# GpSimd takes a subtraction of the weight loads, ScalarE takes the spreading of reciprocal sums

## The chip, the cores and the metric

The kernel runs on one core of one Trainium2 chip. The metric is the device time of one execution in microseconds (us). Three runs of the kernel before took 1221.29 to 1222.41 us, with a median of 1221.92 us; the lower, the better.

## The reference

The reference is an attention with a learned bias, followed by two feed-forward layers. All in fp32:

```python
scores = q @ k.T / sqrt(64) + bias          # 4 batches x 8 heads, 576 x 576
attn   = exp(scores - max) / (sum + 1e-09)  # row by row
x      = (attn @ v)                         # laid out as 2304 tokens x 512
h = x @ w_in;  x = (h * clip(h + 3, 0, 6) / 6) @ w_out           # 2048 wide
x = (sigmoid(x @ w_gate) * (x @ w_val)) @ w_out2                 # 1536 wide
```

The bias is a small network of the distance of two positions. It is made once, for all batches.

## The kernel before, in words

The program has three stages: the table of the bias (to about 60 us of the span), the attention (about 60 to 356 us), and the two feed-forward layers (the rest). The change touches the attention alone, through two pieces of work that sit inside it.

**The attention** goes over 16 units (`NU`): a unit is a pair of heads of one batch. Each unit has 9 steps of 128 query rows, and `slot_of_two` issues two steps at a time. For a step, TensorE forms the scores (L261). VectorE adds the bias and finds each row's minimum (L265, the tile `u`). ScalarE takes the exponential and, with it, the sum of each row (L281, `p` or `pm`, with the sums in `stat`). TensorE transposes the probabilities (L319, L327, L334, `tr`), VectorE and ScalarE by turns copy the result out of PSUM (`ptm`, `ptr`), and TensorE multiplies by the values (L351, L354, `av`).

**The reciprocal sums.** The output comes out transposed, so the sums have to be turned too. `invert` does this in two parts per unit, after step 5 and after step 8. VectorE adds 1e-9 to the sums (L287) and takes reciprocals (L288). GpSimd then repeats each column of reciprocals 64 or 128 times into the tile `spread` (L292, by a multiplication with a column of ones): one instruction of 128x384 in the first part, two of 128x128 in the second. `turn_inv` has TensorE transpose `spread` (L298), and copies the result to `inv`. At L358 VectorE multiplies the output by `inv` and so frees the PSUM tile `av` for the next product.

**Keys and queries.** `prep` splits the next unit's queries and keys into a high part and a remainder. GpSimd makes the high part of the keys (L233) and the remainders of both (L237); ScalarE makes the high part of the queries (L229).

**Weight loads.** The feed-forward weights come as eight-byte numbers and are made into two parts, a high one and a low one, each in a slot of 128x512. `Loader.whole` runs a whole load at once. It is called ten times in the attention (`NPRE` is 10), at every sixth slot. A load is a DMA, then ScalarE's L133, then VectorE's L134, L141, L143 and L145, then `split`: ScalarE rounds the high part into the slot (L151), and VectorE subtracts it to get the low part (L152). Later loads go through `tick`, with the same `split`.

Each engine works through its own queue strictly in order. The framework sets the order inside each queue, from its own estimates of when each operand is ready; it differs from the order of the source.

Of the kernel before, what the change touches and what calls it, by code (L numbers as in the profile page):

```python
# [10 lines left out]
F32 = mybir.dt.float32  # L11
# [3 lines left out]
ALU = mybir.AluOpType  # L15
# [80 lines left out]
def block_kernel(ctx: ExitStack, tc: tile.TileContext, q, k, v, mlp, w_in, w_out, w_gate, w_val, w_out2, dist_d,  # L96
                 rows_d, out):
    nc = tc.nc
# [7 lines left out]
    one = keep.tile([P, 1], F32, name="one")  # L106
# [5 lines left out]
    class Loader:  # L112
# [32 lines left out]
            nc.vector.scalar_tensor_tensor(out=zi, in0=raw[:, :, 0], scalar=29, in1=zi,  # L145
                                           op0=ALU.logical_shift_right, op1=ALU.bitwise_or)

        def split(self, i):
            if i in self.z:
                slot, z = slots[i % NALL], self.z.pop(i)  # L150
                nc.scalar.copy(slot[:, 0], z)  # L151
                nc.vector.tensor_tensor(out=slot[:, 1], in0=z, in1=slot[:, 0].bitcast(F32), op=ALU.subtract)  # L152
                self.done = i + 1

        def whole(self):
            i = self.n
            for stage in (self.dma, self.magnitude, self.assemble, self.split):
                stage(i)
            self.n += 1

        def tick(self):
# [122 lines left out]
    def invert(n, c0, c1):  # L284

        r = sums[n % 3][:, 2 * c0 : min(2 * c1, NSTEP)]
        nc.vector.tensor_scalar(out=r, in0=r, scalar1=1e-9, scalar2=None, op0=ALU.add)  # L287
        nc.vector.reciprocal(r, r)  # L288
        for s0, s1, w in ((0, 6, 64),) if c1 == 3 else ((6, 8, 64), (8, 9, P)):
            o = spread[:, 64 * s0 : 64 * s0 + (s1 - s0) * w].rearrange("p (s w) -> p s w", w=w)  # L290
            i = sums[n % 3][:, s0:s1].unsqueeze(2).to_broadcast(o.shape)
            nc.gpsimd.tensor_tensor(out=o, in0=i, in1=one.unsqueeze(2).to_broadcast(o.shape), op=ALU.mult)  # L292

    def turn_inv(n, c0, c1):

# [70 lines left out]
    for n in range(NU):  # L366
        i = (NSTEP * n + 5) // 2 + 2
# [8 lines left out]
    def slot_of_two(i):  # L376
# [15 lines left out]
        for t in steps(i - 1):  # L392
            n, s = seq[t]
            if s in (5, 8):
                invert(n, s // 6 * 3, s // 6 * 2 + 3)
# [22 lines left out]
    with ExitStack():  # L418
# [215 lines left out]
        for j, (part2, t) in enumerate(todo):  # L634
# [25 lines left out]
            for i in range(NB):  # L660
                o = acc[NB * t + i]
# [32 lines left out]
```

## Time and profile before

| | |
|---|---|
| three runs | 1221.29 to 1222.41 us, median 1221.92 us |
| the profiled execution | 1220.53 us |
| its span, first to last instruction | 1218.8 us |
| TensorE busy | 1193.4 us (98%) |
| VectorE busy | 694.6 us (57%) |
| ScalarE busy | 563.2 us (46%) |
| GpSimd busy | 147.9 us (12%) |
| granted TensorE clock | 1.00 throughout |

Shares are over the whole span. TensorE's busy time is modelled from pipelined matmuls, so 98% does not mean that nothing can be gained. VectorE and ScalarE are much busier in the attention than their averages say, and GpSimd works in the attention alone. PE stands for TensorE, PEld for its loading of weights, DVE for VectorE, ACT for ScalarE, POOL for GpSimd, SP for the queue that issues DMAs.

### The profile page before, as it was taken

Reading aid. Unit: us, or ns where it says so; the run is one execution under the profiler, and the core shown is the slowest. Engines: PE = TensorE matmul, PEld = TensorE weight load, DVE = VectorE, ACT = ScalarE, POOL = GpSimd, SP = SyncE. Lnnn points to the kernel's source line nnn. Section 1 sums busy time; section 2 is a strip of 40 time slices with the busy share of each in tenths; the row PEclk is TensorE's granted clock in tenths of the full one; section 3 lists DMA queues with packets and bytes.
Section 4 is the critical chain, followed back from the end, with each engine's and each line's share of the span. In section 5 each row is a group of like instructions: output and inputs, shape, how many; then the busy total and the mean of one; then the engine's idle time right before and its main releaser. Section 6 shows DMA issues by size and latency. Waiting matters only on the chain.

```text
span 1218.8 us, 18824 instructions
## 1 busy us (share of the span) xinstructions
PE 1193.4 (98%) x7302; PEld 1059.3 (87%) x7302; DVE 694.6 (57%) x1474; ACT 563.2 (46%) x1176; POOL 147.9 (12%) x146
## 2 busy tenths in 40 slices
PE   8999999999999999999999999999999999999998
PEld 4467767676679999999999999999999999999998
DVE  8967887878867665645555555555442454313332
ACT  7977777676755443444443434233322332212221
POOL 0056546546300000000000000000000000000000
PEclk9999999999999999999999999999999999999999
DMA  6743536234312332212122222322210121001000
GB/s 211 251 137 98 179 88 186 86 110 141 98 36 87 104 104 78 67 38 78 49 91 104 104 87 90 126 82 75 79 43 19 61 79 53 31 21 53 26 26 27
DMA packets 36154, 106.78 MB, mean 88 GB/s; under 512 B 3936, under 2 KB 10336, under 8 KB 36064
## 3 DMA queue, kind: packets, MB, share of 16 engines
q1 hardware_dynamic: 36064, 105.57, 26.5%
q8 instruction: 57, 0.93, 0.3%
q14 instruction: 33, 0.27, 0.1%
HBM read 80.78 MB, written 24.77 MB: 87 GB/s over the span
## 4 chain that ended last, share of the span: by engine, by line
PE 85%; DVE 6%; ACT 3%; POOL 2%; issue 2%; DMA 1%; SPq 0%; DVEq 0%; POOLq 0%; ACTq 0%
PE o L573 16%; PE h L511 13%; PE h L509 13%; PE h L510 13%; PE o L630 12%; PE s L261 5%; PE av L351 5%; PE tr L319 4%; PE s L488 2%; PE av L354 1%; DVE x L483 1%; DVE u L265 1%; PE tr L298 1%; ACT p L281 1%; POOL k L237 1%
## 5 line engine op out<-in xcount | busy, mean ns | idle before, releaser
L509 PE MATMUL h<-early,slot 128*128 128x384 f32 x952 | 318.9, 335 | 0.0
L511 PE MATMUL h<-early,slot 128*128 128x384 f32 x952 | 318.8, 335 | 0.0
L510 PE MATMUL h<-early,slot 128*128 128x384 f32 x952 | 318.5, 335 | 0.0
L509 PEld LDWEIGHTS h<-early,slot 128*128 128x128 f32 x952 | 178.7, 188 | 2.6
L510 PEld LDWEIGHTS h<-early,slot 128*128 128x128 f32 x952 | 178.7, 188 | 2.5
L511 PEld LDWEIGHTS h<-early,slot 128*128 128x128 f32 x952 | 178.6, 188 | 0.1
L550 ACT CAST gh<-g 128x384 fp32r<-128x384 f32 x166 | 85.0, 513 | 160.1 <-DVE g L645 119.0
L573 PE MATMUL o<-gh,slot 128*128 128x384 f32 x768 | 156.9, 336 | 1.9 <-ACT raw L309 1.4
L645 DVE TENSOR_TENSOR g<-g,h 128x384 f32<-128x384 f32 x72 | 39.8, 553 | 181.8 <-PE h L511 181.8
L573 PEld LDWEIGHTS o<-gh,slot 128*128 128x128 f32 x768 | 134.2, 188 | 5.7 <-ACT raw L309 4.1
L551 DVE TENSOR_TENSOR gl<-g,gh 128x384 fp32r<-128x384 f32 x166 | 92.1, 558 | 78.4 <-ACT gh L550 76.2
L515 ACT ACTIVATE g<-h,half 128x384 f32<-128x384 f32 x94 | 54.5, 580 | 133.4 <-PE h L511 129.9
L261 PE MATMUL s<-k,q 128*128 128x288 f32 x640 | 113.9, 311 | 1.6 <-POOL k L237 1.0
L281 ACT ACTIVATE p<-u,stat 128x576 f32<-128x576 f32 x128 | 98.7, 772 | 36.1 <-DVE stat L265 35.3
L630 PE MATMUL o<-slot,gh 128*128 128x512 f32 x432 | 111.9, 393 | 0.0
L644 ACT ACTIVATE g<-h 128x384 f32<-128x384 f32 x72 | 35.4, 492 | 163.2 <-PE h L511 163.1
L516 DVE SCALAR_TENSOR_TENSOR g<-g,h 128x384 f32<-128x384 f32 x94 | 51.8, 551 | 96.9 <-ACT g L515 96.9
L265 DVE CUSTOM_DVE_ANT_0 u<-s,bias 128x576 f32<-128x576 f32 x128 | 93.7, 752 | 13.1 <-PE s L261 12.2
L261 PEld LDWEIGHTS s<-k,q 128*128 128x128 f32 x640 | 89.7, 189 | 6.6 <-DVE stat L265 3.0
L630 PEld LDWEIGHTS o<-slot,gh 128*128 128x128 f32 x432 | 80.1, 188 | 13.6 <-issue 0.2
L573 PE MATMUL o<-gl,slot 128*128 128x384 f32 x384 | 88.5, 334 | 0.0
L351 PE MATMUL av<-ptm,vn 128*64 128x288 f32 x512 | 82.8, 419 | 0.5 <-DVE ptm L311 0.5
(98 smaller groups left out, 1509.0 us busy)
## 6 DMA issues: line engine op xcount, KB each, us to landing
raw<-in_part_dram SPq DMA_DIRECT2D x68, 512.0 KB, 3.6
nbias<-p SPq DMA_DIRECT2D x18, 576.0 KB, 3.2
early<-in_part_dram SPq DMA_DIRECT2D x32, 288.0 KB, 4.2
bias<-nbias SPq DMA_DIRECT2D x16, 576.0 KB, 5.9
take<-x SPq DMA_DIRECT2D x12, 768.0 KB, 4.1
vn<-in_part_dram SPq DMA_DIRECT2D x16, 320.0 KB, 3.0
early<-in_part_dram SPq DMA_DIRECT2D x16, 304.0 KB, 3.8
part<-raw SPq DMA_DIRECT2D x12, 384.0 KB, 2.6
```

The lines of the kernel that those rows point to most:

```text
L261: nc.tensor.matmul(ps[:, a, 0:HS], Q[:, q0 : q0 + P], K[:, r, h, HS * a : HS * a + HS], start=(i == 0), stop=(i == len(mm) - 1))
L265: last_u[0] = nc.vector.tensor_tensor_reduce(out=halves(u), in0=ps[:, :, 0:HS], in1=halves(bt), op0=ALU.add, op1=ALU.min, scale=-0.125, sc ...
L281: nc.scalar.activation(probs(t), us.pop(t), AF.Exp, bias=low[n % 2][:, s : s + 1], scale=-1.0, accum_out=sums[n % 3][:, s : s + 1])
L351: nc.tensor.matmul(ps[64 * h : 64 * h + 64, 0:HS], vt[:, 4 * h + g], ptm[:, h, g, cols], start=(g == 0), stop=False)
L509: nc.tensor.matmul(ps[:, 0:TW], wh, XH[:, c], start=(c == 0), stop=False)
L510: nc.tensor.matmul(ps[:, 0:TW], wl, XH[:, c], start=False, stop=False)
L511: nc.tensor.matmul(ps[:, 0:TW], wh, XL[:, c], start=False, stop=(c == 3))
L515: nc.scalar.activation(g, ph, AF.Relu, bias=half, scale=1.0 / 6.0)
L550: nc.scalar.copy(gh, g)
L551: last_g[0] = nc.vector.tensor_tensor(out=gl, in0=g, in1=gh.bitcast(F32), op=ALU.subtract)
L573: nc.tensor.matmul(os[c][:, 0:TW], sl[:, r, P * c : P * c + P], x, start=(first and r == 0 and x is gh), stop=(last and x is gl))
L630: nc.tensor.matmul(os[i], x[:, P * i : P * i + P], sl[:, r], start=(first and x is gh and r == 0), stop=(end and x is gl))
```

## The change

Two operations change engines. In `whole`, the subtraction of the low part (L152) runs on GpSimd; loads through `tick` still use VectorE. In `invert`, the spreading (L292) becomes a plain copy on ScalarE, from the same repeated column.

```diff
-        def split(self, i):
+        def split(self, i, eng=nc.vector):
             if i in self.z:
                 slot, z = slots[i % NALL], self.z.pop(i)
                 nc.scalar.copy(slot[:, 0], z)
-                nc.vector.tensor_tensor(out=slot[:, 1], in0=z, in1=slot[:, 0].bitcast(F32), op=ALU.subtract)
+                eng.tensor_tensor(out=slot[:, 1], in0=z, in1=slot[:, 0].bitcast(F32), op=ALU.subtract)
                 self.done = i + 1
 
         def whole(self):
             i = self.n
-            for stage in (self.dma, self.magnitude, self.assemble, self.split):
+            for stage in (self.dma, self.magnitude, self.assemble):
                 stage(i)
+            self.split(i, nc.gpsimd)
             self.n += 1
...
             i = sums[n % 3][:, s0:s1].unsqueeze(2).to_broadcast(o.shape)
-            nc.gpsimd.tensor_tensor(out=o, in0=i, in1=one.unsqueeze(2).to_broadcast(o.shape), op=ALU.mult)
+            nc.scalar.copy(o, i)
```

One line is added, so lines from L158 on have a number higher by one in the changed kernel (L287 becomes L288, and so on). The DMA queue's order is the same. GpSimd loses 48 instructions and gains 10; ScalarE gains 48; VectorE loses 10. The order in the attention is set anew on TensorE, VectorE, ScalarE and GpSimd. The three places below all lie in the sixth unit.

GpSimd's queue before, as it splits the keys (`k`) and queries (`q`) of the next unit:

```order
L233 TENSOR_TENSOR k_111<-early,one 128x576 x2
L237 TENSOR_TENSOR k_111<-early,k_111 128x576
L292 TENSOR_TENSOR spread<-stat,one 128x384
L237 TENSOR_TENSOR q_109<-early,q_109 64x640
L237 TENSOR_TENSOR k_111<-early,k_111 128x576
L292 TENSOR_TENSOR spread<-stat,one 128x128 x2
L237 TENSOR_TENSOR q_109<-early,q_109 64x576
```

and GpSimd's queue with the change, at the same place:

```order
L152 TENSOR_TENSOR slot_71<-z,slot_71 128x512
L234 TENSOR_TENSOR k_111<-early,one 128x576 x2
L238 TENSOR_TENSOR k_111<-early,k_111 128x576 x2
L238 TENSOR_TENSOR q_109<-early,q_109 64x640
L238 TENSOR_TENSOR q_109<-early,q_109 64x576
L152 TENSOR_TENSOR slot_72<-z,slot_72 128x512
```

The spreads no longer stand behind key and query work; the subtraction of a weight load stands before and after it.

VectorE's queue before, around the first reciprocal of that unit (`ISA u` is L265):

```order
L358 TENSOR_TENSOR x_64<-av,inv 128x288
L311 COPY ptm<-tr 128x4x128
L265 ISA u,stat<-s,bias_106 128x576
L265 ISA stat 128x1
L287 TENSOR_SCALAR stat<-stat 128x6
L265 ISA u,stat<-s,bias_m 128x576
L265 ISA stat 128x1
L288 RECIPROCAL stat<-stat 128x6
L311 COPY ptm<-tr 128x4x128
```

and with the change:

```order
L359 TENSOR_TENSOR x_64<-av,inv 128x288
L288 TENSOR_SCALAR stat<-stat 128x6
L289 RECIPROCAL stat<-stat 128x6
L312 COPY ptm<-tr 128x4x128
L266 ISA u,stat<-s,bias_106 128x576
L266 ISA stat 128x1
L266 ISA u,stat<-s,bias_m 128x576
L266 ISA stat 128x1
L312 COPY ptm<-tr 128x4x128
```

The addition and the reciprocal now stand next to each other, ahead of a copy and two `u`.

ScalarE's queue with the change, at the same place:

```order
L282 ACTIVATE p,stat<-u,stat 128x576 x2
L310 COPY ptm<-tr 128x4x128
L310 COPY ptr<-tr 128x128
L293 COPY spread<-stat 128x384
L282 ACTIVATE p,stat<-u,stat 128x576
L310 COPY ptm<-tr 128x4x128
L282 ACTIVATE pm_113,stat<-u,stat 128x576
L310 COPY ptr<-tr 128x128
L230 CAST q_109<-early 64x640
```

The spread stands between a copy out of PSUM and the next exponential, which waits behind it; the cast of the queries has moved behind `pm`.

## Rows read from the trace of the kernel before

**Rows 1.** The page: span, busy time by engine, chain that ended last by engine.
```profile
span 1218.8 us, 18824 instructions
PE 1193.4 (98%) x7302; PEld 1059.3 (87%) x7302; DVE 694.6 (57%) x1474; ACT 563.2 (46%) x1176; POOL 147.9 (12%) x146
PE 85%; DVE 6%; ACT 3%; POOL 2%; issue 2%; DMA 1%; SPq 0%; DVEq 0%; POOLq 0%; ACTq 0%
```

**Rows 2.** Busy time by stretch: two of four units each, then the attention's end.
```profile
core 0: us, PE busy (x) PEld busy (x) DVE busy (x) ACT busy (x) POOL busy (x), PEclk, DMA share, GB/s
...
111.07:185.12 74.05, 71.18 (x510) 52.87 (x508) 60.14 (x144) 53.70 (x136) 38.97 (x37) 1.00 0.43 125
185.12:259.49 74.37, 70.85 (x510) 52.89 (x508) 59.23 (x144) 53.45 (x136) 38.94 (x37) 1.00 0.41 124
...
334.11:356.00 21.89, 21.89 (x162) 16.00 (x159) 16.60 (x46) 13.95 (x37) 2.47 (x5) 1.00 0.09 29
```

**Rows 3.** Waits of PE and PEld, 60 to 356 us: total us, times, longest.
```profile
PE tr L298 <- POOL spread L292: 5.4, 6, 1.1
PE tr L319 <- DVE ptm L311: 2.5, 3, 1.0
PE tr L319 <- ACT ptm L309: 2.2, 3, 0.7
...
PEld tr L298 <- POOL spread L292: 10.1, 11, 1.7
```

**Rows 4.** Timeline, 163 to 169 us: start us, us, engine, line, what, [idle before].
```profile
163.31 0.25 ACT L309 COPY ptr<-tr 128x128 f32<-128x128 f32 x1
163.84 2.25 POOL L233 TENSOR_TENSOR k<-early,one 128x576 fp32r<-128x576 f32 x2 [7.57 <-PE s L261]
163.88 1.13 DVE L287 TENSOR_SCALAR stat<-stat 128x6 f32<-128x6 f32 x1
164.87 0.78 ACT L281 ACTIVATE p<-u,stat 128x576 f32<-128x576 f32 x1
165.60 0.18 DVE L288 RECIPROCAL stat<-stat 128x6 f32<-128x6 f32 x1
166.05 1.41 POOL L237 TENSOR_TENSOR k<-early,k 128x576 fp32r<-128x576 f32 x1
167.43 0.82 POOL L292 TENSOR_TENSOR spread<-stat,one 128x384 f32<-128x384 f32 x1
168.30 0.20 PEld L298 LDWEIGHTS tr<-ident,spread 128*128 128x128 f32 x2 [1.64 <-POOL spread L292]
```

**Rows 5.** Groups by shape on POOL: count, busy us, mean ns, idle before.
```profile
L237 POOL TENSOR_TENSOR k<-early,k 128x576 fp32r<-128x576 f32 x30 | 42.3, 1419 | 0.7
L292 POOL TENSOR_TENSOR spread<-stat,one 128x128 f32<-128x128 f32 x32 | 13.6, 444 | 6.8 <-DVE stat L288 3.2 <-PE tr L298 3.2
L292 POOL TENSOR_TENSOR spread<-stat,one 128x384 f32<-128x384 f32 x16 | 13.2, 826 | 64.5 <-DVE stat L288 45.0 <-PE tr L319 19.4
```

**Rows 6.** Groups by shape on DVE, 60 to 356 us.
```profile
L287 DVE TENSOR_SCALAR stat<-stat 128x3 f32<-128x3 f32 x16 | 10.9, 683 | 6.0 <-ACT pm L281 4.4 <-POOL k L233 1.5
L134 DVE TENSOR_SCALAR z<-z 128x512 f32<-128x512 f32 x11 | 8.6, 782 | 0.2
L152 DVE TENSOR_TENSOR slot<-z,slot 128x512 fp32r<-128x512 f32 x10 | 8.3, 834 | 0.0
L287 DVE TENSOR_SCALAR stat<-stat 128x6 f32<-128x6 f32 x16 | 6.6, 413 | 0.0
```

**Rows 7.** Timeline, 176 to 181 us: two DVE instructions while POOL stands idle.
```profile
176.26 0.41 DVE L134 TENSOR_SCALAR z<-z 128x512 f32<-128x512 f32 x1
...
180.08 0.16 DVE L287 TENSOR_SCALAR stat<-stat 128x6 f32<-128x6 f32 x1
```

**Rows 8.** Groups by shape on ACT, 60 to 356 us.
```profile
L309 ACT COPY ptr<-tr 128x128 f32<-128x128 f32 x64 | 16.7, 261 | 11.2 <-DVE ptr L311 9.8 <-PE tr L334 1.3
L501 ACT CAST early<-x 128x384 fp32r<-128x384 f32 x4 | 2.0, 519 | 0.0
```

**Rows 9.** The chain, one piece: start us, us, what.
```profile
146.18 1.30 ACT q L229 x2
```

## The prediction

> **What bounds the kernel now.** Start with the page. TensorE is busy for 98% of the span and 85% of the chain that ended last is TensorE's, 6% VectorE's, 3% ScalarE's, 2% GpSimd's [rows 1]. Then look at the stage that the change touches, by busy time in stretches [rows 2]. Four units of the attention, with three weight loads among them, take 74.05 us. TensorE is idle there for 74.05 - 71.18 = 2.87 us, and for 3.52 us in the next four. In the last 21.89 us, where no load runs and GpSimd has little to do, it is never idle. So TensorE is the bound, and what is to be had is the time in which it waits, or in which its pipeline runs thin, because of loads and GpSimd work. In the same stretch VectorE is busy for 60.14 us (81%), ScalarE for 53.70 us (73%), GpSimd for 38.97 us (53%).
>
> Next, who makes TensorE wait: the largest releaser in the attention is GpSimd's spread, 5.4 us on the matmul side in 6 waits, and 10.1 us on the weight side in 11 [rows 3]. The other waits shown are for copies out of PSUM: 2.5 us for VectorE's and 2.2 us for ScalarE's.
>
> Last, one such wait in detail [rows 4]. VectorE's reciprocal ends at 165.60 + 0.18 = 165.78 us. GpSimd is at the keys: two L233 until 166.09 us, then one L237 until 167.46 us. Only then comes the spread, until 168.25 us, and TensorE's transpose has waited 1.64 us when it starts at 168.30 us. The same rows show a second thing. L287, on 768 numbers, takes 1.13 us, and starts and ends with GpSimd's first L233; where GpSimd is idle it takes 0.16 us [rows 7]. L134 takes 0.41 us alone [rows 7] and 0.782 us on average [rows 6]. VectorE thus loses time to GpSimd: (0.683 - 0.16) x 16 = 8.4 us and (0.413 - 0.16) x 16 = 4.0 us on L287, (0.782 - 0.41) x 11 = 4.1 us on L134, 16.5 us for these three groups.
>
> **The change, part by part.**
>
> *Spreads leave GpSimd.* It gives up 13.6 + 13.2 = 26.8 us [rows 5]. What counts is the 5.4 us of TensorE's waits [rows 3]. In the case of [rows 4] ScalarE is free at 163.31 + 0.25 = 163.56 us. A copy that starts with the old reciprocal at 165.78 us and lasts 0.519 us is done at 166.30 us, some 0.4 us before TensorE could use it (168.30 - 1.64 = 166.66 us). So nearly all of this wait can go. But TensorE then comes earlier to the next thing it needs, the copies that ScalarE makes after the spread. I take -4 us, three quarters; the bounds are -5.4 and 0.
>
> *Subtractions leave VectorE.* They are 10 x 0.834 = 8.3 us [rows 6]. This is the last VectorE step of each load, so nothing of the load waits for it there; only the next `u` in VectorE's queue does, and some of those come no sooner because they wait for TensorE's scores. Bounds: 0, if `u` always waits for scores anyway, and -8.3 us, if all of it lies on the path. I take -2 us: of 60 us of VectorE's work per 74 us most has room beside it.
>
> *Subtractions come to GpSimd.* A two-input subtraction of 128x576 takes 1.419 us there [rows 5]. For 128x512, scaling gives 1.26 us and the same row's whole time 1.42 us, so ten cost 12.6 to 14.2 us. GpSimd ends at about 147.9 - 26.8 + 13 = 134 us busy, 9% less. Who waits for the low part? No matmul of the attention; the first use is in the feed-forward layer, behind it. The keys' split stands behind it in GpSimd's queue, but there GpSimd had been idle for 7.57 us before its keys [rows 4]. So the move costs TensorE nothing directly. If the lost 16.5 us of VectorE scale with GpSimd's busy time, 9% is 1.5 us, of which a quarter on the path: -0.4 us. From the order I add one thing: in that unit the addition and reciprocal move ahead of a copy and a `u`, to a time before GpSimd's keys. The 1.13 - 0.16 = 0.97 us lost there recurs every four units, three times in all; half on the path is -1.5 us. Bounds for both together: -4 us (a quarter of 16.5) and +4 us, if subtractions fall on VectorE's work instead.
>
> A rule speaks against this part. The Trainium skill, "SBUF — State Buffer", section "Who interferes with whom", says that VectorE and GpSimd share one pair of ports as an exclusive lock, taken by two-port modes or by instructions with two inputs in SBUF, and that the first to start holds it for its whole length. By it, each GpSimd subtraction can hold VectorE for up to a subtraction's length, and the sum would end near no change (a rival below). The trace agrees that the lock exists (1.13 against 0.16 us), and no row shows where the new subtractions fall.
>
> *Spreads come to ScalarE.* The nearest rows are a 128x384 cast, 0.519 us, and a 128x128 copy, 0.261 us [rows 8]. 16 x 0.519 + 32 x 0.261 = 16.7 us; with 0.519 us for the small ones too it would be 24.9 us, the upper end of the busy time. I take 16.7 us, as the sizes match. ScalarE goes from 53.70 to about 58 us per 74 us. How much is on the path? ScalarE's 3% of the chain is 37 us out of 563.2 us busy [rows 1], 6.5%; of 16.7 us that is 1.1 us. To this comes a new wait: the spread now waits in ScalarE's in-order queue for VectorE's reciprocal, with the next exponential behind it, and TensorE's transposes behind that. In [rows 4] the exponential starts at 164.87 us, 1.31 us after ScalarE was free. If the reciprocal stayed at 165.78 us the exponential would be 165.78 + 0.519 - 164.87 = 1.43 us late. With the reciprocal moved ahead it fits into the gap. I take +2.5 us for both; the bounds are 0 and 16.7 us.
>
> **The sum.** -4 - 2 - 0.4 - 1.5 + 2.5 = -5.4 us. The profiled execution took 1220.53 us, with a span of 1218.8 us, so it would take 1215.1 us. That execution is 1.4 us under the median of the runs, 1221.92 us; against the median the forecast is **1216.5 us**. A measurement of this kernel can tell about 0.2%, or 2.4 us, from no change.
>
> **The rivals.**
>
> *ScalarE becomes the bound (slower).* Place: the exponentials between a spread and TensorE's transposes. The chain already runs through ScalarE at 146.18 us, for 1.30 us of query casts [rows 9], and a spread of 0.519 us stands ahead of them. If half of the 16.7 us is on the path, that is +8.4 us; with the -5.4 us of waits gone in exchange and +1 us of late reciprocals, about +4 us: 1226 us. It decides where the gap before the next exponential is shorter than the spread and the wait for its reciprocal. Against it speaks that ScalarE still has 16 us of 74 idle. Chance 0.21.
>
> *The lock eats the gain (no change).* Each of ten subtractions holds a VectorE instruction for some 0.8 us, half its length and more: +8 us of VectorE's time, as much as it was freed of. Then -2 us, -0.4 us and -1.5 us vanish, the spread's -4 us is set against +2.5 us, and TensorE waits for copies in place of spreads: about 1220.5 us. It is the rule of the Trainium skill cited above, "SBUF — State Buffer". Chance 0.22.
>
> *Much more is freed (faster still).* The whole 5.4 us go; the subtractions count in half, -4 us; and GpSimd's keys, earlier by 0.8 us for each spread gone, stop falling on the load's VectorE steps, -4 us. With ScalarE at no cost that is -13.4 us, 1208.5 us. Chance 0.15.
>
> That the change doesn't do what it says is no case: the order shows both moves.
>
> **How the numbers follow.** The forecast, with its own range from 1213 to 1219.5 us, has 0.42; faster still 0.15; no change 0.22; slower 0.21. So faster by over 0.2% is 0.57, within it 0.22, slower 0.21. The range goes from 1208.5 us, the sum of the gaining bounds that I hold likely, to 1225.5 us, which leaves out about half of the slower case and the tail of the best one.
>
> **What would show it.** Right: TensorE's waits for `spread` fall from 5.4 us below 1.5 us, four units take about 73 us, L287's mean falls, and the feed-forward stage keeps its length. Wrong: waits for ScalarE's copies or for `p` grow by more than 3 us (the slower rival); L134, L141, L143 or L287 grow by more than 0.3 us on average in VectorE's rows (the lock); or ScalarE's spreads take much over 0.5 us.

## The result, and the profile after

The changed kernel takes 1207.91 us (median of 4 runs, 1207.13 to 1208.60) against 1221.61 us for the kernel before, 13.7 us less. The ratio of the two kernels is put at 0.9883, with an interval of 0.9868 to 0.9898. The forecast was 1216.5 us with a range from 1208.5 us. The direction was right and the size was not: two and a half times the forecast, and 0.6 us under the range.

The page of the changed kernel, answering [rows 1]:

```profile
span 1205.4 us, 18764 instructions
PE 1187.5 (99%) x7302; PEld 1057.4 (88%) x7302; DVE 682.1 (57%) x1464; ACT 574.2 (48%) x1224; POOL 133.2 (11%) x108
PE 87%; DVE 6%; ACT 3%; DMA 2%; issue 1%; POOL 0%; SPq 0%; DVEq 0%; ACTq 0%
```

GpSimd's share of the chain that ended last has fallen from 2% to 0%. TensorE's busy time is 5.9 us less, with the same 7302 matmuls.

Where the time went shows in the busy time by stretch, first for the whole attention of the kernel before (60 to 356 us) and then of the changed one (60 to 342 us); columns as in [rows 2]:

```profile
60.00:356.00 296.00, 282.05 (x2013) 210.51 (x2012) 231.63 (x566) 213.29 (x535) 147.06 (x138) 1.00 0.40 119
```

```profile
60.00:342.00 282.00, 276.07 (x2021) 209.53 (x2016) 218.89 (x557) 224.10 (x584) 132.38 (x100) 1.00 0.42 125
```

The whole gain is here: 14 us of attention. From the last output of the attention to the end, both executions take some 855 us. TensorE's idle time falls from 296.00 - 282.05 = 13.95 us to 5.93 us, 8.0 us of it. The other 6.0 us come out of what counts as busy. Two of its groups, first before and then after (count, busy us, mean ns):

```profile
L261 PE MATMUL s<-k,q 128*128 128x288 f32 x640 | 113.9, 311 | 1.6 <-POOL k L237 1.0 <-DVE stat L265 0.3
L351 PE MATMUL av<-ptm,vn 128*64 128x288 f32 x496 | 80.4, 419 | 0.5 <-DVE ptm L311 0.5
```

```profile
L262 PE MATMUL s<-k,q 128*128 128x288 f32 x640 | 112.2, 310 | 2.5 <-POOL k L234 1.2 <-POOL k L238 1.0 <-DVE stat L266 0.3
L352 PE MATMUL av<-ptm,vn 128*64 128x288 f32 x496 | 76.5, 419 | 1.2 <-DVE x L359 0.7 <-DVE ptm L312 0.5
```

A single matmul takes the same time as before. But 640 x 0.311 = 199 us of matmuls lie within 113.9 us of busy time: matmuls overlap, and busy time counts an overlap once. After the change the same matmuls overlap more. That they do so because their operands come in time is likely, but no run shows it by itself.

Four units each, with three weight loads among them, answering [rows 2]:

```profile
110.82:180.45 69.63, 68.72 (x510) 52.45 (x508) 55.81 (x141) 56.07 (x148) 35.79 (x28) 1.00 0.45 133
180.45:250.08 69.63, 68.68 (x510) 52.45 (x508) 55.71 (x141) 56.06 (x148) 35.77 (x28) 1.00 0.45 132
...
319.68:342.00 22.32, 22.32 (x166) 16.37 (x162) 15.50 (x45) 15.24 (x42) 0.00 (x0) 1.00 0.08 28
```

74.05 and 74.37 us have become 69.63 us. VectorE has lost 4.3 us in the first of them and ScalarE gained 2.4 us: both are busy for 80% now.

TensorE's waits, answering [rows 3]:

```profile
PE tr L320 <- ACT inv L310: 1.5, 3, 0.5
PE s L262 <- POOL k L234: 1.2, 1, 1.2
PE s L262 <- POOL k L238: 1.0, 2, 0.7
PE av L352 <- DVE x L359: 0.7, 3, 0.2
PE tr L320 <- DVE ptm L312: 0.6, 3, 0.2
```

The 5.4 us of waits for the spread are gone. The waits that are new, for `inv`, for GpSimd's L234 and for `x`, are 1.5, 1.2 and 0.7 us. The place of [rows 4] in the changed kernel:

```profile
159.76 0.16 DVE L288 TENSOR_SCALAR stat<-stat 128x6 f32<-128x6 f32 x1
...
159.96 0.19 DVE L289 RECIPROCAL stat<-stat 128x6 f32<-128x6 f32 x1
...
160.53 0.52 ACT L293 COPY spread<-stat 128x384 f32<-128x384 f32 x1
...
161.54 2.25 POOL L234 TENSOR_TENSOR k<-early,one 128x576 fp32r<-128x576 f32 x2 [1.90 <-PE s L262]
...
165.44 0.31 PEld L299 LDWEIGHTS tr<-ident,spread 128*128 128x128 f32 x3 [0.44 <-issue]
```

The addition takes 0.16 us where it took 1.13 us, since it now runs 1.8 us before GpSimd's keys. The spread follows 0.38 us after the reciprocal, and is done 4.4 us before TensorE takes it up.

### The profile page after: what moved, and what is told of

It is laid out like the page before. It is cut to its first block, busy times and chain, and to the rows that moved or that the text cites. A ratio compares the mean times of both kernels' runs of the same rounds, so it can differ in the third digit from the quotient of the medians.

```text
span 1205.4 us, 18764 instructions
## 1 busy us (share of the span) xinstructions
PE 1187.5 (99%) x7302; PEld 1057.4 (88%) x7302; DVE 682.1 (57%) x1464; ACT 574.2 (48%) x1224; POOL 133.2 (11%) x108
## 4 chain that ended last, share of the span: by engine, by line
PE 87%; DVE 6%; ACT 3%; DMA 2%; issue 1%; POOL 0%; SPq 0%; DVEq 0%; ACTq 0%
PE o L574 16%; PE h L512 13%; PE h L510 13%; PE h L511 13%; PE o L631 12%; PE s L262 6%; PE av L352 5%; PE tr L320 4%; PE s L489 1%; PE av L355 1%; DVE u L266 1%; DVE x L484 1%; DVE z L143 1%; ACT p L282 1%; PE tr L299 1%
## 5 line engine op out<-in xcount | busy, mean ns | idle before, releaser
L352 PE MATMUL av<-ptm,vn 128*64 128x288 f32 x512 | 78.9, 419 | 1.2 <-DVE x L359 0.7
```

The source lines that it names most:

```text
L352: nc.tensor.matmul(ps[64 * h : 64 * h + 64, 0:HS], vt[:, 4 * h + g], ptm[:, h, g, cols], start=(g == 0), stop=False)
```

## The experiments

Two theories were put up at first. Theory Q: the cost was the spread's place in GpSimd's queue, and ScalarE has room. Theory V: the cost was VectorE's time for the subtraction. Against each other and against the prediction's prices, eleven kernels ran. The changed kernel stands first for comparison.

| run | median us | ratio to before, interval |
|---|---|---|
| the change | 1207.91 | 0.9883, 0.9868 to 0.9898 |
| spread alone | 1214.11 | 0.9948, 0.9928 to 0.9967 |
| subtraction alone | 1213.61 | 0.9938, 0.9923 to 0.9953 |
| change, spread twice | 1211.22 | 0.9924, 0.9909 to 0.9939 |
| change, no addition | 1207.25 | 0.9894, 0.9878 to 0.9911 |
| before, no addition | 1216.91 | 0.9963, 0.9951 to 0.9975 |
| before, no subtraction | 1214.72 | 0.9936, 0.9916 to 0.9957 |
| before, order alone | 1217.79 | 0.9970, 0.9960 to 0.9980 |
| change, spread on VectorE | 1230.32 | 1.0070, 1.0055 to 1.0085 |
| change, subtraction twice | 1209.51 | 0.9900, 0.9884 to 0.9917 |
| change, maximum on GpSimd | 1221.06 | 0.9997, 0.9987 to 1.0006 |
| change, more copies on ScalarE | 1209.80 | 0.9906, 0.9891 to 0.9921 |

### The two parts alone

```diff
-            self.split(i, nc.gpsimd)
+            self.split(i)
```

> The spread goes to ScalarE, the subtraction stays on VectorE. Theory Q (the spread's place in GpSimd's queue was the cost, and ScalarE has room for it): most of the 13.7 us comes from here, 1210 to 1213 us, and TensorE's waits for the spread fall from 5.4 us to under 0.5 us. Theory V (VectorE was the cost: the subtraction lay on its path at each load): here only the 5.4 us of visible waits at most, less what ScalarE loses, 1216 to 1220 us.

```diff
-            nc.scalar.copy(o, i)
+            nc.gpsimd.tensor_tensor(out=o, in0=i, in1=one.unsqueeze(2).to_broadcast(o.shape), op=ALU.mult)
```

> The subtraction goes to GpSimd, the spread stays on GpSimd. Theory Q: 1218 to 1222 us, as the subtraction's 12.8 us on GpSimd push the spreads back further and eat what VectorE gains. Theory V: 1210 to 1214 us. If the two parts add up, the gains of this run and of the one with the spread alone sum to 13.7 us; if the sum is clearly smaller, the parts help each other.

The first gave -7.2 us, the second -7.7 us (medians against 1221.31 us). The first lies between the two theories, the second where theory V had it. So neither theory holds alone, and each part brings far more than it was put at. The two sum to 14.9 us against 13.7 us, which the intervals of some 2 us on each cannot tell apart. Four units in each, first with the spread alone, then with the subtraction alone:

```profile
186.20:257.90 71.70, 70.58 (x510) 52.81 (x508) 57.21 (x146) 56.49 (x148) 32.10 (x25) 1.00 0.43 129
```

```profile
181.10:252.00 70.90, 68.91 (x510) 52.49 (x508) 54.91 (x143) 53.35 (x136) 42.67 (x40) 1.00 0.42 130
```

Against the 74.37 us of the same stretch before, that is 2.7 and 3.5 us per four units, 6.2 us together, where both at once bring 74.37 - 69.63 = 4.7 us. So in the steady part, the units between the first few and the last, they overlap.

With the spread alone, 2.4 of the 2.7 us are idle time of TensorE (3.52 us before, 1.12 us now). That is not only the waits for the spread. The waits for copies out of PSUM fell too, over the attention from 2.5 + 2.2 [rows 3] + 1.7 us to 2.5 us; the third of these before, then the two that are left:

```profile
PE tr L334 <- ACT ptm L309: 1.7, 2, 0.8
```

```profile
PE tr L320 <- ACT ptm L310: 1.3, 1, 1.3
PE tr L320 <- DVE ptm L312: 1.2, 3, 0.4
```

And VectorE, with the same 1474 instructions, is busy for 685.5 us in place of 694.6 us: the first additions of a unit take 0.163 us there in place of 0.413 us. How much of the gain comes through this was not told apart.

The overlap of the two parts can be seen in the waits. With the subtraction alone the spread is still on GpSimd, and yet:

```profile
PE tr L299 <- POOL spread L293: 1.6, 2, 1.0
```

5.4 us of waits for the spread have become 1.6 us without the spread being touched. The new order accounts for it, at the same place as before:

```profile
158.80 1.28 POOL L152 TENSOR_TENSOR slot<-z,slot 128x512 fp32r<-128x512 f32 x1 [4.28 <-ACT slot L151]
160.32 0.16 DVE L288 TENSOR_SCALAR stat<-stat 128x6 f32<-128x6 f32 x1
160.52 0.19 DVE L289 RECIPROCAL stat<-stat 128x6 f32<-128x6 f32 x1
160.88 0.83 POOL L293 TENSOR_TENSOR spread<-stat,one 128x384 f32<-128x384 f32 x1 [0.80 <-PE tr L320]
162.10 2.25 POOL L234 TENSOR_TENSOR k<-early,one 128x576 fp32r<-128x576 f32 x2 [0.40 <-PE s L262]
```

With the subtraction off VectorE the framework puts the reciprocal ahead, the spread becomes ready before GpSimd's keys, and goes ahead of them. The next run, which makes this order by hand, has the same 1.6 us.

### The order alone

In the kernel before, subtraction and spread where they were:

```diff
...
+        first = [seq[t] for t in steps(i - 1) if seq[t][1] == 5 and seq[t][0] % 2]
+        for n, s in first:
+            invert(n, 0, 3)
         for t in steps(i):
-            scores(t)
+            if first:
+                with tc.issue_after(recip[0].ins):
+                    scores(t)
+            else:
+                scores(t)
...
```

Here `recip[0]` is the last reciprocal, and the later `invert` skips these.

> The kernel before, with subtraction and spread where they were, but with the first addition and reciprocal of every second unit queued on VectorE ahead of the two u of the next steps, as the changed kernel has them. Theory O (moving the subtraction gains by the new order more than by VectorE's time): the three waits of 1.64 us for the spread and the three held additions of 1.13 us go, 3 x 1.2 + 3 x 0.97 = 6.5 us at most: 1214.5 to 1218 us. Theory T (it gains by VectorE's time): 1219.5 to 1222 us.

1217.79 us, just inside theory O: 3.7 us, without a single instruction changing its engine, about half of what the subtraction brings alone. The rest, some 4 us, is left for VectorE's own time and for other changes of the order; these two were not told apart.

### What GpSimd's hold on VectorE costs

```diff
-        nc.vector.tensor_scalar(out=r, in0=r, scalar1=1e-9, scalar2=None, op0=ALU.add)
```

> The kernel before without the addition of 1e-9 alone (it changes nothing in fp32, as a sum is at least 1). The 32 additions took 17.5 us of VectorE there, 12.4 us of it beside GpSimd's key and query work. It prices the stretches in which GpSimd holds VectorE up at this one place. If they lie on the path, as three pieces of 1.13 us seem to: 1214 to 1218 us. If the other work covers them: 1219 to 1222 us.

> The changed kernel without the addition of 1e-9 to the sums (a sum is at least 1, as the largest probability is exp(0), so in fp32 the addition changes nothing). It takes away 32 small VectorE instructions, 13.8 us busy in the changed kernel, of which only 32 x 0.165 = 5.3 us is work and 8.4 us is spent while GpSimd holds on to its keys. If these stretches lie on the path (three of 1.15 us are pieces of the chain that ended last): 1203 to 1206 us. If they are covered: 1207 to 1208.5 us.

The same edit brings 4.6 us in the kernel before and cannot be told from nothing in the changed one. In the kernel before it removes additions held up by GpSimd, and with them the delay of the reciprocals. The waits for the spread fall to 0.8 us there too, while those for copies grow:

```profile
PE tr L318 <- DVE ptm L310: 3.8, 3, 1.3
PE tr L333 <- ACT ptm L308: 2.5, 3, 0.8
...
PE tr L297 <- POOL spread L291: 0.8, 2, 0.6
```

In the changed kernel the additions are still held (0.618 us on average for the second ones, against 0.165 us free), and three of them are pieces of the chain that ended last. Taking them out gains nothing that can be measured: a piece of that chain is not a price.

### What the moved work costs where it now runs

The spread made twice, `nc.scalar.copy(o, i)` on two lines:

> The changed kernel with each spread made twice on ScalarE, one straight after the other: another 16.2 us of ScalarE's time at the durations of the changed kernel's rows (16 x 0.516 + 32 x 0.296 = 17.7 us). It prices the term that was put at +2.5 us for a first set of copies. If ScalarE's time is off the path, as the changed kernel's trace suggests: 1208 to 1210 us. If it is on the path at 15% or more, the price that the prediction took: 1210.5 us and over.

A second set of copies costs 1211.22 - 1207.91 = 3.3 us, which is the second expectation. The copies last 17 us, of which it is a fifth; as they overlap their neighbours, ScalarE's busy time grows only from 574.2 to 585.7 us, 11.5 us. It is the price of a further set, with ScalarE already at 80% in the steady part. What the first set cost is not shown: no run takes the spread off GpSimd without putting it on another engine.

The subtraction made twice on GpSimd:

> The changed kernel with each of GpSimd's ten subtractions made twice, one straight after the other: 12.8 us more on GpSimd. It prices the subtraction on GpSimd by itself, beside the run that leaves it out. If GpSimd's time and its hold on VectorE cost nothing there: 1207 to 1209 us. If each holds VectorE for some 0.8 us, as the rival of the lock has it: 1211 us and over.

1209.51 us lies between the two expectations: 1.6 us more, with intervals that overlap. Four units take 0.3 us more than the 69.63 us of the changed kernel:

```profile
143.93:213.82 69.89, 68.91 (x510) 52.48 (x509) 56.57 (x140) 55.93 (x148) 39.61 (x30) 1.00 0.44 132
```

The second subtractions do hold VectorE: the first additions of a unit take 0.437 us on average, against 0.241 us in the changed kernel. The third run leaves the subtraction out altogether, in the kernel before:

```diff
...
-            for stage in (self.dma, self.magnitude, self.assemble, self.split):
+            for stage in (self.dma, self.magnitude, self.assemble):
                 stage(i)
+            self.split(i, False)
...
```

> The kernel before with the ten subtractions of the low part left out during the attention (the low parts of these ten slots are zeros that GpSimd writes before the attention). Against the run with the subtraction on GpSimd it prices what GpSimd's ten subtractions cost: if nothing, the same time within 1 us, 1212.5 to 1214.5 us; if they hold up VectorE or the keys, this run is the faster by 2 us or more, under 1211.6 us.

1214.72 us, no better than with GpSimd doing it (1213.61 us). But the total settles little. Its four executions go from 1211.42 to 1220.49 us; in the profiled one, of 1220.49 us, the granted clock averages 0.993, and the zeros that GpSimd writes first hold a step of VectorE:

```profile
1.38 4.72 POOL L445 MEMSET slot<- 128x512 f32 x10
4.20 1.99 DVE L449 TENSOR_SCALAR early<-early 128x144 f32<-128x144 f32 x1 [2.77 <-DMA early<-in_part_dram]
```

In the kernel before that step takes 0.29 us. The granted clock is 0.85 between 10 and 20 us, and GpSimd's first work of the attention starts at 73.05 us, where it started at 68.24 us. The steady part is the fair comparison. Four units at the full clock:

```profile
220.66:291.55 70.89, 68.92 (x510) 52.49 (x509) 54.92 (x140) 53.38 (x135) 38.84 (x36) 1.00 0.43 130
```

That is the 70.90 us of the run with the subtraction on GpSimd. In the steady part, then, GpSimd's subtractions cost nothing that shows.

### The spread on the third engine

```diff
-            nc.scalar.copy(o, i)
+            nc.vector.tensor_copy(o, i)
```

> The changed kernel, but with the spread on VectorE in place of ScalarE. Theory Q (what counts is that the spread leaves GpSimd's queue): any engine with room will do, 1207 to 1211 us. If VectorE's time is what bounds the stage, its some 10 us of copies (48 copies at 0.16 to 0.3 us, the shorter and longer of its own rows of such sizes) and its waits for GpSimd give back half of the gain or more: 1213 us and over.

22 us slower than the change and slower than the kernel before. "Any engine with room will do" falls. Its groups on VectorE show a cause, beside ScalarE's in the changed kernel:

```profile
L293 DVE COPY spread<-stat 128x128 f32<-128x128 f32 x32 | 30.9, 1003 | 0.5
L293 DVE COPY spread<-stat 128x384 f32<-128x384 f32 x16 | 6.2, 386 | 0.4
```

```profile
L293 ACT COPY spread<-stat 128x384 f32<-128x384 f32 x16 | 8.3, 516 | 0.0
L293 ACT COPY spread<-stat 128x128 f32<-128x128 f32 x32 | 7.9, 296 | 2.6 <-DVE stat L289 2.5
```

On VectorE the small copies take 1.003 us on average, the three times larger ones 0.386 us. Most of the small ones fall beside GpSimd's keys and queries and take up to 1.46 us; most of the large ones fall where GpSimd is idle. On ScalarE the small copies also fall beside GpSimd's work, and none takes more than 0.31 us.

The 22 us are not all this hold. The granted clock averages 0.993 over the span of 1228.4 us, where the changed kernel has 1.00. With levels of 1 and one half that is some 17 us at the lower one, worth up to 8.6 us by an estimate from these two numbers. The two were not separated.

### Two tries at a faster kernel

Both start from the changed kernel without the addition. The first moves one more step of each load:

```diff
-                nc.vector.tensor_scalar(out=z, in0=z, scalar1=2.0**-15, scalar2=None, op0=ALU.max)
+                eng.tensor_scalar(out=z, in0=z, scalar1=2.0**-15, scalar2=None, op0=ALU.max)
...
```

with `eng` GpSimd in `whole`, VectorE in `tick`.

> The changed kernel without the addition of 1e-9, and with one more VectorE step of each load in the attention, the maximum at L134, on GpSimd. VectorE loses eleven steps of 0.61 us on average (11 x 0.417 us alone), GpSimd gains ten of about 1.2 us, and the load's later steps start later. If VectorE's time is still what the loads cost: 1203 to 1206 us. If the loads' price is spent: 1206.5 to 1208 us. If the earlier step delays the load and puts more of GpSimd's work across VectorE's two-input steps: 1209 us and over.

1221.06 us: all of the gain is lost. The maximum is the load's first step on VectorE, and VectorE's next step waits for it in VectorE's in-order queue:

```profile
152.05 1.48 POOL L134 TENSOR_SCALAR z<-z 128x512 f32<-128x512 f32 x1
153.56 0.43 DVE L141 TENSOR_SCALAR z<-z 128x512 int32<-128x512 int32 x1 [3.79 <-POOL z L134]
153.99 0.46 DVE L359 TENSOR_TENSOR x<-av,inv 128x288 f32<-128x288 f32 x1
154.36 0.41 DVE L312 COPY ptm<-tr 128x256 f32<-128x256 f32 x1
...
154.84 1.11 PE L320 MATMUL tr<-ident,p 128*128 128x128 f32 x4 [3.41 <-DVE ptm L312]
```

GpSimd came to the maximum only after its queries and keys. VectorE stood for 3.79 us with copies out of PSUM behind it, and TensorE for 3.41 us; three such waits make 10 us, and a lower granted clock behind them adds to it (last section). The subtraction is the load's last step, so VectorE never waits for it. That is the difference between the two moves.

The second try:

```diff
-PT_EVAC = "VAVAVAVAA"
+PT_EVAC = "VAVAVAAAA"
...
```

> The changed kernel without the addition of 1e-9, and with one more of nine copies out of PSUM on ScalarE in place of VectorE (16 copies of 0.685 us leave VectorE, 11 us; ScalarE gains 16 x 0.58 = 9.3 us). If VectorE is the scarcer of the two: 1203 to 1206 us. If ScalarE's room is used up, as the doubled spread suggests (3.3 us for 17.7 us more): 1207 to 1211 us.

1209.80 us, 2.6 us worse than the kernel it starts from (1207.25 us). There ScalarE is busy for 56.27 of 69.60 us in the steady part, 81%, and VectorE for 52.72 us, 76%. ScalarE has nothing more to give. No version beat the changed kernel by more than can be measured.

## Why the prediction was wrong in size

**Spreads leave GpSimd, -4 us, and come to ScalarE, +2.5 us.** Together -1.5 us; alone they measured -7.2 us. The wait was found rightly, and it went. The step that failed is the bound: "the bounds are -5.4 and 0." TensorE's recorded waits for the spread were taken as the most that could come back. Moving the spread alone brought back more than that, as waits for copies out of PSUM fell too and VectorE was busy for 9.1 us less. For the whole change, only 8.0 of the 14 us that the attention got shorter were idle time of TensorE; 6.0 us lay in its busy time. ScalarE's price was sought in its share of the chain and in the wait for the reciprocal. Its busy time grew by 574.2 - 563.2 = 11.0 us and not by 16.7 us, as neighbouring instructions overlap there. What the first set of copies cost stays open; the second set cost 3.3 us.

**Subtractions leave VectorE, -2 us.** Alone they measured -7.7 us, near the bound of -8.3 us. The step that failed is the list of followers: "only the next `u` in VectorE's queue does". The addition and the reciprocal were missed in this term. With the subtraction gone they moved ahead, and with them the spread.

**The order, -1.5 us, and the lock, -0.4 us.** The order of [rows 4] alone, in the kernel before, is worth 3.7 us, as it ends the held addition and TensorE's 1.64 us of waiting at one stroke; part of this the prediction had counted with the spreads. The lost time on VectorE was scaled with GpSimd's busy time (9% less). It does not follow it: GpSimd's busy time fell by 10%, and the 16.5 us lost in the three groups, worked out in the same way, became 11.0 us. Which instruction happens to stand beside GpSimd's work decides. The first additions of a unit fell from 0.413 us to 0.241 us on average, L134 from 0.782 to 0.625 us, while L143 rose from 0.924 to 1.027 us:

```profile
L143 DVE SCALAR_TENSOR_TENSOR z<-raw,z 128x512 int32<-128x512 int32 x11 | 11.3, 1027 | 0.2
L288 DVE TENSOR_SCALAR stat<-stat 128x3 f32<-128x3 f32 x16 | 9.9, 618 | 6.0 <-ACT pm L282 6.0
...
L134 DVE TENSOR_SCALAR z<-z 128x512 f32<-128x512 f32 x11 | 6.9, 625 | 0.0
...
L288 DVE TENSOR_SCALAR stat<-stat 128x6 f32<-128x6 f32 x16 | 3.9, 241 | 0.0
```

**Subtractions on GpSimd, nothing.** Right, as far as the runs can tell: leaving them out makes the steady part no shorter than moving them, and a second set costs 1.6 us by the medians. Each takes 1.28 us, near the lower of the two estimates.

**The rivals.** "Much more is freed" had a chance of 0.15 and named 1208.5 us. Its time came, its terms only in part: the 5.4 us went, but the subtraction measured -7.7 us and not -4 us, and VectorE's load steps did not all gain, as L143 shows. That the number fits so closely is partly luck. The lock's rival fell for the subtraction, but the hold itself is real: the small copies of the spread on VectorE show it. ScalarE, the bound of the slower rival, is the next limit, as the doubled spread and the extra copies suggest.

**The signs.** TensorE's waits for the spread went, L287's means fell, and the feed-forward stage kept its length, as forecast; none of the signs of being wrong came. Only the four units, 69.63 us in place of about 73 us, show that the gain was put too low.

What stays open is how the subtraction's 7.7 us divide, beyond the 3.7 us of the order.

## What to carry to other kernels

When an engine with long instructions delivers a small result, look at what stands ahead of it in that queue, and at what the move does to the order on the others: here two small instructions that moved forward brought 3.7 us by themselves. The waits for one releaser are no upper bound for what moving it gains, nor is the bounding engine's idle time: here 6.0 of 14 us came out of its busy time. Give a slow engine the last step of a chain; an earlier step puts the wait into someone else's queue.

## What was not expected of the hardware

128x128 copies took 1.003 us on average on VectorE and 128x384 copies 0.386 us, in one kernel, for where they stood beside GpSimd's work.

The other concerns TensorE's clock. In the try with the maximum on GpSimd, the stretches around TensorE's 3.41 us wait read (columns as in [rows 2]; the granted clock is the last number but two):

```profile
151.00:154.80 3.80, 0.43 (x4) 0.19 (x2) 1.24 (x4) 0.22 (x2) 2.52 (x2) 1.00 0.69 173
154.80:159.00 4.20, 4.16 (x21) 3.02 (x21) 3.45 (x8) 1.89 (x5) 0.00 (x0) 0.59 0.26 60
159.00:163.00 4.00, 4.00 (x30) 2.98 (x27) 2.48 (x7) 2.44 (x8) 1.12 (x1) 1.00 0.00 0
```

TensorE was busy for 0.43 us of 3.80 us, and then had a granted clock of 0.59 on average over the next 4.20 us, most of it at the lower of its two levels, 1.2 GHz of 2.4 GHz. So this wait cost twice: the wait, and the matmuls behind it. Over the whole span of 1219.0 us the granted clock averages 0.993, which by the estimate made above is worth up to 8.5 us. In the changed kernel all stretches shown stand at 1.00.
